# Turning the softmax sums of one row block, with two weight conversions placed later

## The chip, the cores and the metric

The kernel runs on one core of a Trainium2 chip. The core has five engines with a queue each: TensorE (PE in the rows; PEld is its loading of weights), VectorE (DVE), ScalarE (ACT), GpSimd (POOL) and SyncE (SP), which issues most of the DMAs. Each engine takes its instructions in the order in which they stand in its queue, and waits on semaphores for the others. The metric is the device time of one execution in microseconds; the median of three runs of the kernel before is 1201.55.

## What is computed

Capped attention, a gated MLP over its rows, and a mixture of experts with one expert a token. The part that matters here is the attention and the start of the MLP (all inputs are float32; `cap` is 30):

```python
scores = scale * np.matmul(q, k.transpose(0, 1, 3, 2))     # q, k, v: 4 x 12 x 448 x 64
scores = cap * np.tanh(scores / cap)
scores = scores - np.max(scores, axis=-1, keepdims=True)
attn = np.exp(scores)
attn = attn / (np.sum(attn, axis=-1, keepdims=True) + 1e-09)
x = np.matmul(attn, v)                                     # then 1792 rows of 12 * 64 = 768

rms = np.sqrt(np.mean(x * x, axis=-1, keepdims=True) + 1e-06)
xn = x / rms * rms_g
g = xn @ w_gate                                            # 768 x 1536
silu = g * (1.0 / (1.0 + np.exp(-g)))
x = (silu * (xn @ w_val)) @ w_out                          # 1536 x 768
```

After that come the routing of the 1792 rows to 8 experts with 224 places each, and two layers an expert; the change does not touch them.

## The kernel before

**Tiles and units.** The rows are worked in four blocks b of 448 (S), one for each element of the batch. The 12 heads of a block go in pairs: m counts 24 pairs, six a block, and a pair fills 128 partitions with two heads of 64. Scores are made transposed: 112 keys (T) on the partitions, 448 queries along the row, for both heads (a). A pair has four such key tiles; a unit u is two of them, m, i = divmod(u, 2). `scores(m, i)` makes the scores of a unit on PE into one of two PSUM tiles s_, and ACT makes tanh and exp of them into t_. `av(m, i)`, one unit later, multiplies v by t_ into a PSUM tile PS. All matmuls of the MLP split each float32 operand in a high and a low part (xh, xl; wh, wl) and sum three products (`mm3`).

**Sums of p.** The softmax needs 1 over the sum of t_ over all keys. For the first block of rows (m below 6) PE makes the sums by matmuls with ones beside those with v. From m = 6 on DVE adds the four tiles t_ into `ps` (L247, L250), and `fin(m)` sums its 112 partitions with two matmuls by ones, `ffb<-ps,ones`. These leave the sum of a head on all of its 64 partitions. DVE inverts the 128x448 tile (L270) and multiplies PS by it into oT (L274). The squares of oT, added up in ssq, give rms of a block.

**Weights.** The MLP's weights come as 64-bit floats in 18 pieces, 12 for gate and value columns and 6 for the output. They are made float32 by integer operations: a conversion (`convert`) handles half a piece: ACT makes u_ (L380), then DVE runs four operations (L381, L384 to L386). u_ has two buffers. `split_piece` then makes wh on ACT (L420) and wl on DVE (L422). `convert` runs ahead of need by `ahead`, at most three pieces (NR). A finished piece is also stored for the later blocks, which load it instead of converting it.

**Stages.** Stage 1 runs units 0 to 13, that is, block 0 and the start of block 1, with ten conversions in units 1 to 10; the order of PE's instructions is fixed there (`pinned`). Then `split_x(0)` makes xh and xl of block 0 and the body begins: `Driver.merge` mixes units of the next block with `gateval(0)`, which goes over 12 blocks of 128 gate and value columns (f), and with 16 conversions. A gate block takes two PSUM tiles, the gate's (j = 0) with six products by k, and then the value's (j = 1); DVE and ACT make silu of them. `rms` and `rms_rows` put 1/rms as RB behind the first products. Next come `second()`, the output projection of block 0 (`outproj`, whose results leave as xr) and the gates of block 1, and so on. In each, the order on an engine is set when the program is built: a scheduler with a timeline of its own puts what it takes to be ready first. PSUM for PS, gate tiles, sums and transposes is four tiles called ffb.

Of the kernel before, what the change touches and what calls it, by code (L numbers as in the profile page):

```python
# [10 lines left out]
F32 = mybir.dt.float32  # L11
F32R = mybir.dt.float32r
BF = mybir.dt.bfloat16
I32 = mybir.dt.int32
AF = mybir.ActivationFunctionType
# [4 lines left out]
B, H, S, D = 4, 12, 448, 64  # L20
# [3 lines left out]
T = 112  # L24
NQ = S // T
# [14 lines left out]
KD = DM // 128  # L40
KF = DF // 128
# [78 lines left out]
def program(tc, acap, general, qT, kT, v, wf64, g, wg2, w1, w2, out):  # L120

    nc = tc.nc
    drv = Driver()
    pe = Pe(tc)
    with ExitStack() as ctx:
# [6 lines left out]
        ident = const.tile([128, 128], F32, name="ident")  # L132
        make_identity(nc, ident)
        ones = const.tile([128, D], F32, name="ones")
# [32 lines left out]
        ff = ctx.enter_context(tc.tile_pool(name="ff", bufs=4, space=PSUM))  # L167
# [3 lines left out]
        wcv = actx.enter_context(tc.tile_pool(name="wcv", bufs=2))  # L171
        raw = actx.enter_context(tc.tile_pool(name="raw", bufs=3))
        pt = actx.enter_context(tc.tile_pool(name="pt", bufs=5))
        sm = actx.enter_context(tc.tile_pool(name="sm", bufs=2))
        ps_s = actx.enter_context(tc.tile_pool(name="ps_s", bufs=2, space=PSUM))

        RAW, MX, PT, PS, SU, OT, SQ = {}, {}, {}, {}, {}, {}, {}
# [50 lines left out]
        def halves(o_, w, x, first, last):  # L228

            for a in range(2):  # L230
                pe.matmul(o_[a * D:(a + 1) * D], w(a), x[:, a], start=first, stop=last, skip_group_check=True)

        def av(m, i):


            ts = [PT.pop((m, 2 * i + j)) for j in range(2)]
            if i == 0:
                PS[m] = ff.tile([128, S], F32, name="ffb")
                SU[m] = ff.tile([128, S], F32, name="ffb") if m < H // 2 else ts[0]
            for j, t_ in enumerate(ts):  # L240
                halves(PS[m], lambda a: RAW[m][2][:, a, 2 * i + j], t_, i + j == 0, i + j == 2)
            for j, t_ in enumerate(ts):
                if m < H // 2:
                    halves(SU[m], lambda a: ones[:T], t_, i + j == 0, i + j == 2)
                elif i + j == 1 and i == 0:
                    u_ = sm.tile([T, 2, S], F32, name="ps")
                    nc.vector.scalar_tensor_tensor(u_, SU[m], gcol[:T], t_, op0=OP.add, op1=OP.add)  # L247
                    SU[m] = u_
                elif i:
                    nc.vector.tensor_tensor(SU[m], SU[m], t_, op=OP.add)  # L250
            if i:
                RAW.pop(m)
                drv.later(1, lambda: fin(m))

        def square(b, o, x):
            if b:
                nc.scalar.activation(o, x, AF.Square)
            else:
                nc.gpsimd.tensor_tensor(o, x, x, op=OP.mult)

        def fin(m):
            b, c = divmod(m, H // 2)
            if c == 0:
                OT[b] = oTp.tile([128, KD, S], F32, name="oT")
            o_, u_ = PS.pop(m), SU.pop(m)
            rc = sm.tile([128, S], F32, name="rc")
            if b:
                p_ = ff.tile([128, S], F32, name="ffb")
                halves(p_, lambda a: ones[:T], u_, True, True)
                nc.vector.reciprocal(rc, p_)  # L270
            else:
                nc.vector.tensor_scalar(rc, u_, gsum, None, op0=OP.add)
                nc.vector.reciprocal(rc, rc)
            nc.vector.tensor_tensor(OT[b][:, c], o_, rc, op=OP.mult)  # L274
            x = OT[b][:, c]
            if c == 0:
                SQ[b] = ftmp.tile([128, S], F32, name="ssq", bufs=2)
                square(b, SQ[b], x)
            else:
                t_ = ftmp.tile([128, S], F32, name="sqt", tag="tmp", bufs=3)  # L280
                square(b, t_, x)
                nc.vector.tensor_tensor(SQ[b], SQ[b], t_, op=OP.add)

        def gate_constants():
# [10 lines left out]
        C_ATT = 24 * 2.24 * W_ATT  # L295

        def attention():
            load_pair(0, nc.sync)
            load_pair(1, nc.sync)
            load_half(NI - 1)  # L300
            gate_constants()
            for u in range(NH + 1):
                m, i = divmod(u, 2)
                if 0 < u < H - 1:
                    ahead(u - 1)
                if u in (H // 3, H // 2):
                    split_piece(u // 2 - 2)
                if m < NH // 2:
                    if i == 0 and general:
                        row_max(m)  # L310
                    if i == 0 and m + 2 < NH // 2:
                        load_pair(m + 2, nc.gpsimd)
                    scores(m, i)
                if u:
                    z, j = divmod(u - 1, 2)
                    av(z, j)
                yield 4.48
# [34 lines left out]
        HC = 6  # L352
# [15 lines left out]
        def convert(upto):  # L368

            while nh[1] <= min(upto, 2 * NP - 1):  # L370
                z, hf = divmod(nh[1], 2)
                load_half(nh[1])
                r_ = I64.pop(nh[1])
                if hf == 0:
                    WT[z] = wraw.tile([128, 12, 128], F32, name="r_", bufs=NR)
                u_ = wcv.tile([128, HC, 128], BF, name="u_", bufs=2)
                d_ = WT[z][:, hf * HC:(hf + 1) * HC]
                di = d_.bitcast(I32)
                hw, lw = r_[:, :, :, 1], r_[:, :, :, 0]
                tc.keep_in_program_order(nc.scalar.activation(u_, hw.bitcast(F32), AF.Abs))  # L380
                first = nc.vector.tensor_scalar(di, hw, 3, 0x3FFFFFF8, op0=OP.logical_shift_left,  # L381
                                                op1=OP.bitwise_and)
                tc.keep_in_program_order(first)
                nc.vector.scalar_tensor_tensor(di, hw, -0x40000000, di, op0=OP.bitwise_and, op1=OP.bitwise_or)  # L384
                nc.vector.scalar_tensor_tensor(di, lw, 29, di, op0=OP.logical_shift_right, op1=OP.bitwise_or)
                nc.vector.scalar_tensor_tensor(d_, u_, TINY, d_, op0=OP.is_ge, op1=OP.mult)  # L386
                load_half(nh[1] + NI)
                nh[1] += 1
                if hf:
                    nc.sync.dma_start(wf32[z], WT[z])  # L390
                    nxt[0] += 1
# [5 lines left out]
        def conversion(n):  # L397
            for _ in range(n):
                ahead(nh[1])
                yield 1  # L400
# [31 lines left out]
        def gateval(b):  # L432
            xh, xl = XN[b]
            for f in range(KF):
                z = GV0[b] + f
                split_piece(z + 1)
                wh, wl, r_ = WT.pop(z)
                order = [(j, k) for j in range(2) for k in range(KD)]
                if b == B - 2 and f == KF - 1:

                    order.sort(key=lambda jk: jk[1])
                ps = {}
                for i, (j, k) in enumerate(order):
                    if j not in ps:
                        ps[j] = ff.tile([128, S], F32, name="ffb")
                    mm3(ps[j], wh[:, 6 * j + k], wl[:, 6 * j + k], xh[k], xl[k], k, KD)
                    if f == 0 and i == 1 and b < B - 1:
                        rms(b)
                    if f == 0 and i == KD - 1:
                        rms_rows(b)  # L450
                    if i % 2:
                        yield 1.14
                    if (j, k) == (0, KD - 1):
                        o = ps[0]
                        th = ftmp.tile([128, S], F32, name="th", tag="tmp", bufs=3)
                        nc.vector.tensor_tensor(o, o, RB[b], op=OP.mult)
                        nc.scalar.activation(th, o, AF.Tanh, scale=0.5)
                        nc.vector.scalar_tensor_tensor(th, th, 1.0, o, op0=OP.add, op1=OP.mult)
                pool = tp if b < B - 1 else TP[0]
                th_ = pool.tile([128, S], F32R, name="tfh")  # L460
                tl_ = pool.tile([128, S], F32R, name="tfl")
                TF[b, f] = (th_, tl_)
                nc.vector.scalar_tensor_tensor(th, th, 0.5, ps[1], op0=OP.mult, op1=OP.mult)
                nc.scalar.activation(th_, th, AF.Copy)  # L464
                nc.gpsimd.tensor_tensor(tl_, th, th_.bitcast(F32), op=OP.subtract)  # L465
        C_GV = KF * 6 * 1.14
# [112 lines left out]
        att = attention()  # L579
# [1 line left out]
        drv.merge((islice(att, H + 2), 1))  # L581
        pe.pinned = False
        split_x(0)
        drv.merge((islice(att, H), C_ATT), (gateval(0), C_GV), (conversion(16), 16))
        split_x(1)
        drv.merge((islice(att, H), C_ATT), (second(), C_GV + C_OP), (conversion(20), 20))
        split_x(2)
# [391 lines left out]
```

## Time and profile before

| | |
|---|---|
| median of three runs (lowest to highest) | 1201.55 us (1195.22 to 1203.76) |
| profiled execution | 1201.41 us, span 1199.5 us |
| PE busy (matmuls) | 1126.7 us, 94% of the span |
| DVE busy | 770.9 us, 64% |
| ACT busy | 567.8 us, 47% |
| POOL busy | 207.4 us, 17% |
| mean granted clock of PE | 0.975 |

The shares are means over the whole span. The change touches the first 300 us, so the stages of that part are to be read by themselves: how many matmuls PE issues in a stretch, how long DVE is busy in it, and what ended PE's waits. Where a row counts several matmuls as one line, x4 means four passes through the array; a float32 matmul shows as two.

### The profile page before, as it was taken

What the parts mean: (1) busy time and instruction counts of PE and PEld (TensorE: products, weight loads), DVE (VectorE), ACT (ScalarE), POOL (GpSimd) and SP (SyncE); (2) the same over time, 40 slices, a digit from 0 to 9 for tenths busy, and PEclk for the clock granted to TensorE, in tenths of its full rate; (3) what the DMA queues carried; (4) which work ended last, traced back from release to release, by engine and by line L of the source; (5) the groups of instructions that cost most, each with busy time, mean ns of one, the idle gap of its engine ahead of it and who ended that gap; (6) DMA issues with size and microseconds to landing.
All of it is one profiled execution on the core that took longest, in us unless ns stands there. A gap on an engine that the chain in (4) does not pass through costs nothing. (4 is left out here: it accounts for less than half of the span.)

```text
span 1199.5 us, 14960 instructions
## 1 busy us (share of the span) xinstructions
PE 1126.7 (94%) x5830; PEld 867.8 (72%) x5830; DVE 770.9 (64%) x1118; ACT 567.8 (47%) x753; POOL 207.4 (17%) x188
## 2 busy tenths in 40 slices
PE   6988999989999999999899999999996999999995
PEld 2326666646677776577677899777775999999995
DVE  3996999998555665446575544255654666666661
ACT  5884667574344465543353333211002556666552
POOL 1222332210012221001112233311101101011000
PEclk8998999999999999999999999999998999999998
DMA  7661355547423333332232233410005666766640
GB/s 247 196 241 37 128 194 191 207 151 268 148 101 102 103 102 113 112 113 78 80 105 80 79 106 106 184 51 16 24 16 161 230 232 229 241 231 230 230 159 26
DMA packets 46113, 169.40 MB, mean 141 GB/s; under 512 B 5424, under 2 KB 16688, under 8 KB 46032
## 3 DMA queue, kind: packets, MB, share of 16 engines
q1 hardware_dynamic: 38896, 142.19, 35.2%
q0 software_dynamic: 7136, 26.16, 6.8%
q8 instruction: 48, 0.79, 0.3%
q14 instruction: 33, 0.27, 0.1%
HBM read 143.16 MB, written 25.17 MB: 140 GB/s over the span
## 5 line engine op out<-in xcount | busy, mean ns | idle before, releaser
L98 PE MATMUL ffb<-xh,wh 128*128 128x448 f32 x576 | 218.9, 380 | 7.0 <-DVE rc L270 4.5
L98 PE MATMUL ffb<-xl,wh 128*128 128x448 f32 x576 | 214.3, 372 | 0.0
L98 PE MATMUL ffb<-xh,wl 128*128 128x448 f32 x576 | 213.8, 371 | 0.0
L812 DVE TENSOR_TENSOR el<-mr,eh 128x1536 fp32r<-128x1536 f32 x64 | 112.5, 1758 | 72.8 <-ACT eh L811 72.8
L465 POOL TENSOR_TENSOR tfl<-th,tfh 128x448 fp32r<-128x448 f32 x48 | 103.6, 2158 | 293.3 <-ACT tfh L464 293.3
L98 PEld LDWEIGHTS ffb<-xh,wh 128*128 128x128 f32 x576 | 109.5, 190 | 43.3 <-issue 13.3
L98 PE MATMUL ffb<-tfh,wh 128*128 128x448 f32 x288 | 117.1, 406 | 4.7 <-ACT wh L420 3.2
L98 PE MATMUL ffb<-xg,eh 128*128 128x448 f32 x384 | 120.5, 375 | 0.0
L98 PEld LDWEIGHTS ffb<-xl,wh 128*128 128x128 f32 x576 | 109.6, 190 | 12.4 <-issue 2.8
L98 PEld LDWEIGHTS ffb<-xh,wl 128*128 128x128 f32 x576 | 109.4, 190 | 11.2 <-issue 0.7
L98 PE MATMUL ffb<-tfh,wl 128*128 128x448 f32 x288 | 108.7, 378 | 2.9 <-DVE wl L422 2.9
L811 ACT ACTIVATE eh<-mr 128x1536 fp32r<-128x1536 f32 x64 | 94.9, 1486 | 30.2 <-PE ffb L98 11.6
L98 PE MATMUL ffb<-tfl,wh 128*128 128x448 f32 x288 | 108.6, 377 | 0.0
L98 PE MATMUL ffb<-xg,el 128*128 128x224 f32 x384 | 91.9, 268 | 0.0
L98 PEld LDWEIGHTS ffb<-xg,el 128*128 128x128 f32 x384 | 73.7, 192 | 1.5
L98 PEld LDWEIGHTS ffb<-xg,eh 128*128 128x128 f32 x384 | 69.1, 190 | 3.8
L98 PEld LDWEIGHTS ffb<-tfh,wh 128*128 128x128 f32 x288 | 56.8, 197 | 19.8 <-issue 7.5
L98 PE MATMUL l<-el,hh 128*112 128x384 f32 x256 | 65.9, 338 | 0.0
L98 PE MATMUL l<-eh,hh 128*112 128x384 f32 x256 | 65.4, 342 | 0.0
L98 PE MATMUL l<-eh,hl 128*112 128x384 f32 x256 | 65.4, 336 | 0.0
L98 PEld LDWEIGHTS ffb<-tfh,wl 128*128 128x128 f32 x288 | 56.0, 195 | 9.7 <-DVE wl L422 3.4
L270 DVE RECIPROCAL rc<-ffb 128x448 f32<-128x448 f32 x18 | 53.1, 2953 | 13.1 <-PE ffb L98 13.1
(1164 smaller groups left out, 1957.7 us busy)
## 6 DMA issues: line engine op xcount, KB each, us to landing
mr<-w SPq DMA_DIRECT2D x64, 768.0 KB, 5.7
ih<-wf SPq DMA_DIRECT2D x36, 768.0 KB, 4.7
xrow<-xr SPq DMA_DIRECT2D x24, 224.0 KB, 2.5
gr<-wf SPq DMA_DIRECT2D x18, 256.0 KB, 2.9
wf<-r__191 SPq DMA_DIRECT2D x1, 768.0 KB, 5.6
wf<-r__264 SPq DMA_DIRECT2D x1, 768.0 KB, 7.6
wf<-r__341 SPq DMA_DIRECT2D x1, 768.0 KB, 3.2
wf<-r__418 SPq DMA_DIRECT2D x1, 768.0 KB, 3.3
```

Source lines behind the costliest of these rows:

```text
L98: return self.pin(self.tc.nc.tensor.matmul(*a, **k))
L270: nc.vector.reciprocal(rc, p_)
L465: nc.gpsimd.tensor_tensor(tl_, th, th_.bitcast(F32), op=OP.subtract)
L811: nc.scalar.activation(wh, r_, AF.Copy)
L812: sb = nc.vector.tensor_tensor(wl, r_, wh.bitcast(F32), op=OP.subtract)
```

## The change

Four things are changed in the first two stages.

1. For pairs 6 to 11 (`turned`, the second block of rows) the sums are taken with the tiles' columns turned onto partitions: `invert` runs eight matmuls that have 112 columns of ps as weights and one column of ones as data, into eight spare columns of the PSUM tile PS (which is now 512 wide). DVE inverts the 112x8 result, ACT spreads each number over 64 elements (`rw`, 112x512), and two steps later `fin` turns the four 112x128 parts back by PE transposes; ACT copies them to rc. The multiplication by rc stays. All other pairs of later blocks keep the old way.
2. The conversions in stage 1 end after unit 8 instead of 10, the merge of the body asks for 20 instead of 16, and u_ has three buffers.
3. The first gate block of block 0 goes by k with both tiles side by side, so that each xh, xl serves gate and value at once; rms and rms_rows stand accordingly later.
4. The square of pair 5 moves from GpSimd to ACT.

```diff
+        def turned(m):
+            return H // 2 <= m < H
+
+        def turned_sums(m, t_):
+            for i in range(NQ):
+                for a in range(2):
+                    z = S + 2 * i + a
+                    pe.matmul(PS[m][:T, z:z + 1], t_[:, a, i * T:(i + 1) * T], ones[:T, :1], start=False, stop=True,
+                              skip_group_check=True)
...
             if i == 0:
-                PS[m] = ff.tile([128, S], F32, name="ffb")
+                PS[m] = ff.tile([128, 512], F32, name="ffb")
...
-                drv.later(1, lambda: fin(m))
+                drv.later(1, partial(invert if turned(m) else fin, m))
...
-            if b:
+            if m >= H // 2 - 1:
                 nc.scalar.activation(o, x, AF.Square)
...
+        def invert(m):
+            turned_sums(m, SU[m])
+            ri = sm.tile([T, NQ, 2], F32, name="ri")
+            nc.vector.reciprocal(ri.rearrange("p i a -> p (i a)"), PS[m][:T, S:S + 2 * NQ])
+            SU[m] = sm.tile([T, NQ, 2 * D], F32, name="rw", bufs=1)
+            nc.scalar.activation(SU[m].rearrange("p i (a d) -> p i a d", a=2),
+                                 ri[:, :, :, None].to_broadcast([T, NQ, 2, D]), AF.Copy)
+            drv.later(2, partial(fin, m))
...
+                p_ = ff.tile([128, S], F32, name="ffb")
+                if turned(m):
+                    for i in range(NQ):
+                        pe.transpose(p_[:, i * T:(i + 1) * T], u_[:, i], ident[:T, :T])
+                    nc.scalar.activation(rc, p_, AF.Copy)
+                else:
+                    halves(p_, lambda a: ones[:T], u_, True, True)
+                    nc.vector.reciprocal(rc, p_)
...
-                if 0 < u < H - 1:
+                if 0 < u < H - 3:
                     ahead(u - 1)
...
-                u_ = wcv.tile([128, HC, 128], BF, name="u_", bufs=2)
+                u_ = wcv.tile([128, HC, 128], BF, name="u_", bufs=3)
...
-                if b == B - 2 and f == KF - 1:
+                late = b == 0 and f == 0
+                if late or (b == B - 2 and f == KF - 1):
                     order.sort(key=lambda jk: jk[1])
...
-                    if f == 0 and i == 1 and b < B - 1:
+                    if f == 0 and i == (2 * KD - 3 if late else 1) and b < B - 1:
                         rms(b)
-                    if f == 0 and i == KD - 1:
+                    if f == 0 and i == (2 * KD - 2 if late else KD - 1):
                         rms_rows(b)
...
-        drv.merge((islice(att, H), C_ATT), (gateval(0), C_GV), (conversion(16), 16))
+        drv.merge((islice(att, H), C_ATT), (gateval(0), C_GV), (conversion(20), 20))
```

The scheduler moves instructions with this. On PE at the seam of stage 1 and the body, behind the last scores of unit 13 (in these rows xh_638, xl_639 are the parts for k = 0 before, xh_620, xl_621 in the change; the numbers only tell tiles apart), before:

```order
L98 MATMUL ffb<-t__598,v__460 64x448 x2
L98 MATMUL ffb<-t__599,v__460 64x448 x2
L98 MATMUL s__668<-q__531,k__532 112x448 x2
L98 MATMUL ffb<-t__625,v__460 64x448 x2
L98 MATMUL s__669<-q__531,k__532 112x448 x2
L98 MATMUL ffb<-t__626,v__460 64x448 x2
L98 MATMUL ffb<-ps,ones 64x448 x2
L98 MATMUL ffb<-xh_638,wh 128x448
L98 MATMUL ffb<-xl_639,wh 128x448
```

and now:

```order
L98 MATMUL ffb<-t__580,v__460 64x448 x2
L98 MATMUL ffb<-xh_620,wh 128x448
L98 MATMUL ffb<-xl_621,wh 128x448
L98 MATMUL ffb<-xh_620,wl 128x448
L98 MATMUL ffb<-xh_624,wh 128x448
L98 MATMUL ffb<-xl_625,wh 128x448
L98 MATMUL ffb<-xh_624,wl 128x448
L98 MATMUL ffb<-t__581,v__460 64x448 x2
L98 MATMUL ffb<-xh_628,wh 128x448
L98 MATMUL ffb<-xl_629,wh 128x448
```

Before, all gate products stand behind the sums of pair 6 (`ffb<-ps,ones`). Now twelve stand ahead of the scores of unit 14, the first eight of them in these rows, and five more follow before pair 6's sums.

Further on in the same stretch PE now has the way back of pair 6 (rw) and the rows of rms behind the last products of the first gate block, with scores of units 15 to 17 among them, and the second gate block's first product behind:

```order
L98 MATMUL ffb<-xh_640,wl 128x448
L98 MATMUL s__781<-q__513,k__514 112x448 x2
L98 MATMUL s__782<-q__513,k__514 112x448
L101 MATMUL ffb<-ident,rw 128x112 x4
L98 MATMUL s__782<-q__513,k__514 112x448
L98 MATMUL s__875<-q__568,k__569 112x448 x2
L98 MATMUL ffb<-ones,ssq 112x1 x4
L98 MATMUL s__876<-q__568,k__569 112x448 x2
L98 MATMUL s__985<-q__568,k__569 112x448 x2
L101 MATMUL ffb<-ident,RR 128x112 x4
L98 MATMUL ffb<-xh_620,wh 128x448
```

Before, only the scores s of unit 15 stood in this stretch; those of s__875, s__876 and s__985 came behind gate products of the next block.

On DVE at the start of the output projection, ahead of the first xr. Before (r__1609 is the 13th piece of the weights, r__1705 the 14th):

```order
L381 TENSOR_SCALAR r__1705<-ih 128x768
L250 TENSOR_TENSOR ps<-ps,t__1937 112x896
L384 SCALAR_TENSOR_TENSOR r__1705<-ih,r__1705 128x768
L250 TENSOR_TENSOR ps<-ps,t__1938 112x896
L422 TENSOR_TENSOR wl<-r__1609,wh 128x1536
L381 TENSOR_SCALAR r__1705<-ih 128x768
L385 SCALAR_TENSOR_TENSOR r__1705<-ih,r__1705 128x768
L506 TENSOR_TENSOR xr<-ffb,RR 112x512
```

and now (r__1795 is the 14th piece, r__1925 the 15th, r__2043 the 16th):

```order
L450 TENSOR_TENSOR wl<-r__1795,wh 128x1536
L409 TENSOR_SCALAR r__2043<-ih 128x768
L414 SCALAR_TENSOR_TENSOR r__1925<-u__1926,r__1925 128x768
L409 TENSOR_SCALAR r__1925<-ih 128x768
L412 SCALAR_TENSOR_TENSOR r__2043<-ih,r__2043 128x768
L263 TENSOR_TENSOR ps<-ps,t__2021 112x896
L535 TENSOR_TENSOR xr<-ffb,RR 112x512
```

Before, the 13th piece was split and the 14th in the making when the first xr came; now the 14th is split, and the 15th and 16th are in the making. Behind about 340 us the order of the engines is as before, but for one pair that changes places on DVE.

## Rows read from the trace of the kernel before

**Rows 1.** Stretches: us; busy us (instructions) PE, PEld, DVE, ACT, POOL; PEclk, DMA, GB/s.
```profile
54.84:85.50 30.66, 25.48 (x120) 8.12 (x120) 30.10 (x32) 24.95 (x26) 5.08 (x8) 1.00 0.71 248
85.50:110.20 24.70, 21.47 (x95) 12.78 (x94) 18.42 (x21) 13.49 (x17) 7.43 (x9) 0.86 0.27 91
...
97.50:110.20 12.70, 12.70 (x59) 10.42 (x58) 7.35 (x9) 5.33 (x8) 2.18 (x3) 0.81 0.18 54
110.20:245.00 134.80, 131.56 (x601) 88.26 (x601) 128.82 (x141) 87.05 (x102) 39.91 (x26) 0.99 0.48 166
245.00:340.00 95.00, 86.22 (x391) 56.60 (x388) 73.81 (x83) 47.05 (x53) 7.35 (x11) 0.96 0.56 186
345.00:445.00 100.00, 100.00 (x479) 76.20 (x478) 59.30 (x61) 48.55 (x58) 26.77 (x20) 1.00 0.31 105
```

**Rows 2.** Waits, 7 to 97 us, ACT: who waited for whom, us, times, longest.
```profile
ACT u__522 L380 <- DVE r__418 L386: 1.7, 1, 1.7
...
ACT u__419 L380 <- DVE r__341 L386: 1.5, 1, 1.5
```

**Rows 3.** Timeline (start, us, instruction, [idle <-releaser]): first scores of units 8, 12, 13.
```profile
54.84 1.01 PE L98 MATMUL s__464<-q__308,k__309 64*112 64x448 f32 x4 [0.17 <-ACT t__433 L219]
...
80.65 1.01 PE L98 MATMUL s__592<-q__458,k__459 64*112 64x448 f32 x4
...
85.50 1.01 PE L98 MATMUL s__619<-q__458,k__459 64*112 64x448 f32 x4
```

**Rows 4.** Timeline: a conversion on DVE to the next one's start, then the seam.
```profile
75.64 0.55 DVE L381 TENSOR_SCALAR r__491<-ih 128x768 int32<-128x768 int32 x1
76.22 0.96 DVE L384 SCALAR_TENSOR_TENSOR r__491<-ih,r__491 128x768 int32<-128x768 int32 x1
...
79.16 0.55 DVE L381 TENSOR_SCALAR r__491<-ih 128x768 int32<-128x768 int32 x1
...
95.83 1.76 PE L98 MATMUL ffb<-ps,ones 112*64 112x448 f32 x4 [3.23 <-DVE ps L250]
...
96.97 0.62 DVE L282 TENSOR_TENSOR ssq<-ssq,sqt 128x448 f32<-128x448 f32 x1 [0.82 <-POOL sqt L259]
97.51 0.68 DVE L348 SCALAR_TENSOR_TENSOR xl<-oT,gt,xh 128x448 fp32r<-128x448 f32 x1
```

**Rows 5.** Timeline: the first product of the second gate block.
```profile
110.19 0.36 PE L98 MATMUL ffb<-xh,wh 128*128 128x448 f32 x1
```

**Rows 6.** DVE's reciprocals: groups of 97.5 to 244.5 us, and a timeline row.
```profile
L270 DVE RECIPROCAL rc<-ffb 128x448 f32<-128x448 f32 x6 | 17.7, 2950 | 0.6 <-PE ffb L98 0.6
...
4.49 0.15 DVE L139 RECIPROCAL qs<-acap 128x1 f32<-128x1 f32 x1
```

**Rows 7.** Timeline of PE: the matmuls of rms and the transposes of its rows.
```profile
329.91 0.85 PE L98 MATMUL ffb<-ones,ssq 128*112 128x1 f32 x8
330.62 0.45 PE L98 MATMUL ffb<-xh,wh 128*128 128x448 f32 x1
...
337.83 0.57 PE L101 MATMUL ffb<-ident,RR 112*128 112x112 f32 x4
```

**Rows 8.** ACT's copies: a timeline row, and a group of 97.5 to 244.5 us.
```profile
108.30 0.53 ACT L336 ACTIVATE RB<-ffb 128x448 f32<-128x448 f32 x1
...
L257 ACT ACTIVATE sqt<-oT 128x448 f32<-128x448 f32 x5 | 2.9, 571 | 7.9 <-DVE oT L274 7.9
```

**Rows 9.** Waits, 245 to 340 us, PE: us, times, longest.
```profile
PE ffb L98 <- ACT wh L420: 3.2, 2, 1.6
PE ffb L98 <- DVE wl L422: 2.9, 1, 2.9
PE ffb L98 <- DVE th L458: 1.5, 1, 1.5
```

More of the change, by code (lines that the diff above doesn't have):

```diff
@@ L237, in av @@
             if i == 0:
-                PS[m] = ff.tile([128, S], F32, name="ffb")
+                PS[m] = ff.tile([128, 512], F32, name="ffb")
                 SU[m] = ff.tile([128, S], F32, name="ffb") if m < H // 2 else ts[0]
             for j, t_ in enumerate(ts):
-                halves(PS[m], lambda a: RAW[m][2][:, a, 2 * i + j], t_, i + j == 0, i + j == 2)
+                halves(PS[m][:, :S], lambda a: RAW[m][2][:, a, 2 * i + j], t_, i + j == 0, i + j == 2)
             for j, t_ in enumerate(ts):
@@ L252, in av, with square @@
                 RAW.pop(m)
-                drv.later(1, lambda: fin(m))
-        def square(b, o, x):
-            if b:
+                drv.later(1, partial(invert if turned(m) else fin, m))
+        def square(m, o, x):
+            if m >= H // 2 - 1:
                 nc.scalar.activation(o, x, AF.Square)
@@ L264, in fin @@
                 OT[b] = oTp.tile([128, KD, S], F32, name="oT")
-            o_, u_ = PS.pop(m), SU.pop(m)
+            o_, u_ = PS.pop(m)[:, :S], SU.pop(m)
             rc = sm.tile([128, S], F32, name="rc")
[L267 to L271, printed above, removed]
+            if b == 0:
                 nc.vector.tensor_scalar(rc, u_, gsum, None, op0=OP.add)
                 nc.vector.reciprocal(rc, rc)
+            else:
[4 more added lines that the diff above has]
+                    nc.scalar.activation(rc, p_, AF.Copy)
+                else:
+                    halves(p_, lambda a: ones[:T], u_, True, True)
+                    nc.vector.reciprocal(rc, p_)
             nc.vector.tensor_tensor(OT[b][:, c], o_, rc, op=OP.mult)
@@ L277, in fin @@
                 SQ[b] = ftmp.tile([128, S], F32, name="ssq", bufs=2)
-                square(b, SQ[b], x)
+                square(m, SQ[b], x)
             else:
                 t_ = ftmp.tile([128, S], F32, name="sqt", tag="tmp", bufs=3)
-                square(b, t_, x)
+                square(m, t_, x)
                 nc.vector.tensor_tensor(SQ[b], SQ[b], t_, op=OP.add)
```

## The prediction

> **What bounds the kernel now.** I read the time by stages first, then what ended the waits in each, then single rows.
>
> The profiled execution took 1201.41 us, of which the span is 1199.5; the median of the three runs is 1201.55, so the sum below can be set against either. TensorE (PE) is busy for 94% of the span, but the table by stages shows where it is not well fed [rows 1]. From 345 to 445 us, where VectorE (DVE) has work for only 59 us, PE issues 479 matmuls in 100.0 us, 0.209 us each; I use this as the price of one in this mix. At that price the 601 matmuls of 110.2 to 245 us need 125.6 us and take 134.8 (9.2 lost), and the 391 of 245 to 340 us need 81.7 and take 95.0 (13.3 lost). In those two stretches DVE is busy 128.8 and 73.8 us, and late in the first stage, from 54.84 to 85.5 us, 30.1 of 30.7. So up to about 300 us DVE works nearly without a break, and PE waits for what it makes late. From 340 us on the order of the engines is the same in both kernels but for one swap on DVE, so what is won by then stays won.
>
> How DVE's lateness reaches PE in the first stage: ACT, about to make u_ for a conversion, stood waiting for a u_ buffer, which is freed by the last DVE operation of the conversion two before. There are four such waits of 1.5 to 1.7 us [rows 2]. Behind it in ACT's queue stand the tanh and exp of the scores, and PE has only two score buffers. Units of attention follow each other at 4.85 us where nothing waits (80.65 to 85.50), but the four from 54.84 to 80.65 took 25.8 us instead of 19.4 [rows 3]. At the seam between the stages PE then waits 3.23 us for p's sums, with the first gate products queued behind, and the last xl is made only at 97.51 [rows 4]. PE's granted clock is 0.81 in the mean there, so at its lower level (1.2 GHz) for part of the time [rows 1].
>
> **The change, part by part.**
>
> *Two conversions later, three u_ buffers, products by k.* A conversion costs DVE 3.5 us (75.64 to 79.16) [rows 4] and ACT 0.9. Two of them leave the first stage: 7.0 us of DVE. DVE's work there is unbroken, so the last xl is ready near 97.5 - 7.0 = 90.5 us. With three buffers and no conversion behind the eighth, ACT has none of the four waits, and unit 13's scores start near 54.84 + 5 x 4.85 = 79.1 instead of 85.50. From there to the first product of the second block of gate columns, 110.19 [rows 5], PE takes 24.7 us for 95 matmuls [rows 1], which at 0.209 are 19.9. In the order of the change the stretch also holds 12 matmuls of scores that came later (2.5 us), and the first turned pair (+1.0, below): 23.4 us. Gate products stand where the 3.23 us wait was. What is new is that PE needs ACT's copy of the turned sums, its copy back and RB, one behind the other; I allow 3 us for these. The stretch ends at 79.1 + 23.4 + 3 = 105.5: 4.7 us sooner and 2.5 us of scores further on, 7.2 in all. If the clock falls as it does before (0.81 over 12.7 us costs 2.4), it is 4.8. I take 6; the bounds are 4.8 and, without the 3 us, 10. The conversions land where DVE has room, busy 7.35 of 12.7 us from 97.5 to 110.2 [rows 1]; without that room they would cost DVE 7 us in the stage behind. SyncE's queue carries the same loads two conversions later, with nobody new waiting for them. One square goes from GpSimd, where it held DVE's ssq up by 0.82 us [rows 4], to ACT for 0.57 us [rows 8].
>
> *Six pairs turned.* DVE loses six reciprocals of 2.95 us [rows 6] and gains six of 112x8. The small one has no row; it lies between 0.15 us (a reciprocal of one column [rows 6]) and 2.95, and with eight columns against 448 I take 0.2. That is 16.5 us of DVE, 13.8 of them behind 110 us. PE loses two matmuls with ones, four passes or 0.84 us, and gains eight one-column matmuls and four transposes. The nearest row is rms: four one-column matmuls, 8 passes, 0.71 us to the next matmul [rows 7]. So 16 passes take 1.42. Four transposes show 0.57 with their tail [rows 7]; I take 0.45. Net +1.0 us a pair, 6 in all. ACT gains two copies, near 0.53 and 0.65 us (0.57 for 448 elements, scaled to 512) [rows 8], 1.2 us a pair; it is busy 87 of 134.8 us [rows 1], which hides them unless PE waits for one.
>
> The price of the one-column passes is where the gain turns. The Trainium skill (TensorE: Matmul & The Clock Gate, section Back-to-back issue gap) gives matmuls of 1 to 64 columns a floor of about 25 ns; by that the 16 passes would cost 0.4 us, a pair nothing net, and the result would be near 1184. The trace shows 0.71/8 = 89 ns a pass, and I go by the row.
>
> *The body, 110 to 245 us.* DVE needs 128.8 - 13.8 and some 2 us of the moved conversions for which the room does not suffice: 117 us. PE needs 125.6 + 5 x 1.0 = 130.6. So PE becomes the bound, and the most to be had is 134.8 - 130.6 = 4.2 us. Not all of PE's waits will go: weights, p's sums and PSUM tiles still come in turn. I take half, 2 us. If nothing of the 9.2 is won back, the stage is 5 us longer.
>
> *The output projection, 245 to 340 us.* PE waits for wh, wl and th, 7.6 us in four waits [rows 9], and the mean clock of 0.96 [rows 1] costs up to 3.8. Both come from DVE being late with conversions. In the changed order DVE has converted one piece more before the first xr and begun the next two, and it arrives with some 10 us less behind it. I take 3.5 us; the bounds are 0 (the wait moves to the next late piece) and 9.
>
> **Sum.** 6 + 2 + 3.5 = 11.5 us; 1201.4 - 11.5 = 1189.9, say 1190.
>
> **Rivals.**
>
> *PE is full.* For: in the body PE reads as busy 131.6 of 134.8 us [rows 1]. Taken at its word there are 3.2 us to win and 5.0 to add; with all its present waits the body is 5 us longer. Against: 479 matmuls in 100 us read as full too, at a higher rate. Then 6 - 5 + 1 are won: 1199.5. The Trainium skill (Trainium Kernel Development and Optimization, section Performance Expectations) calls matmul busy time a bad metric, because matmuls are pipelined. By that, the trace agrees: 601 in 134.8 and 479 in 100.0 us both read as nearly full.
>
> *All of it.* The seam gives 9, the body 4.2, the projection 8: 1180. For: 22.5 us are lost in the two stretches, and one-column passes below 89 ns would help. Against: PE, in order, has waits that are not DVE's.
>
> *The way back is too long (slower).* PE meets the transposes in order, with gate products queued behind, before ACT has written the turned sums: DVE's small reciprocal may stand behind a wl, ACT's copy behind tanh, exp or wh, six times over. At a wait like that of the seam, 3.23 us [rows 4], this costs 19 us, and 2.4 each for the clock behind it, 14 more: 1190 + 33 = 1223. The gain is gone from 11.5/6 = 1.9 us a pair, without the clock. Against: the order sets scores or gate products between the sums and the way back.
>
> *Nothing moves.* The waits of the first stage pass to DVE's next late result; 2 of the 6 stay and the rest cancels: about 1200.
>
> **Chances.** The forecast, 1184 to 1196: 0.50. PE full: 0.18. All of it: 0.17. Nothing moves: 0.07. Slower: 0.08. Less than 1% (1189.5 to 1213.6) can hardly be told from no change here. Half of the forecast's own range lies below 1189.5, so faster is 0.25 + 0.17 = 0.42; slower by over 1% is 0.06, and within 1% 0.52. The range leaves out the slower case and the lower part of "all of it": 1181 to 1201.
>
> **What would show it.** Units 9 to 13 at 4.85 us and no wait for u_ in the first stage; the second gate block's first product near 105.5 us; eight one-column matmuls at 1.4 us, and transposes of rw with no wait ahead of them; body and projection shorter by 2 and 3.5 us; a constant shift from 340 us on. It would be wrong if PE waited ahead of most of those transposes, if the one-column matmuls were well off 1.4 us, or if DVE still had no break before 300 us.

## The result, and the profile after

The changed kernel takes 1184.13 us (median of four runs, 1181.26 to 1189.33) beside 1200.63 for the kernel before on the same chip: a ratio of 0.9866, interval 0.9839 to 0.9894, so 12.7 to 19.3 us less. On a second occasion it was 0.9890 (0.9861 to 0.9919). The profiled execution, 1189.33 us, is the slowest of the four, 12.0 us of span below before's.

The page's head, and the table by stages in the columns of [rows 1], cut at the same places of the program (unit 8, unit 13, first product of the second gate block, first product of the output projection, then a stretch in which both kernels run the same order):

```profile
PE 1130.0 (95%) x5926; PEld 876.9 (74%) x5926; DVE 754.1 (64%) x1118; ACT 572.6 (48%) x766; POOL 206.8 (17%) x187
```
```profile
53.49:78.46 24.97, 24.66 (x123) 8.29 (x121) 24.55 (x25) 21.93 (x23) 5.18 (x8) 1.00 0.73 247
78.46:108.23 29.77, 24.26 (x123) 13.91 (x121) 25.31 (x31) 19.66 (x23) 9.67 (x8) 0.94 0.32 98
108.23:243.61 135.38, 134.88 (x675) 96.38 (x673) 122.10 (x152) 91.64 (x115) 36.67 (x27) 0.99 0.58 195
243.61:332.00 88.39, 88.39 (x409) 59.70 (x410) 67.42 (x73) 45.94 (x52) 7.02 (x11) 1.00 0.50 164
332.00:432.00 100.00, 100.00 (x478) 76.23 (x477) 58.96 (x61) 48.82 (x57) 26.59 (x20) 1.00 0.32 106
```

DVE has breaks now (122.1 of 135.4 us in the body, where [rows 1] had 128.8 of 134.8), and PE has none: in the projection it is busy for the whole stretch at full clock. Behind it nothing moved, 478 matmuls in 100 us as before. From 110 to 340 us a single wait of PE is left, in the columns of [rows 9]:

```profile
PE ffb L98 <- DVE th L487: 0.5, 1, 0.5
```

The seam, to be laid beside [rows 3], [rows 4] and [rows 5]. The first scores of units 8, 12 and 13; the first gate product; the sums of pair 6 (x16), rw, and the rows of rms (RR):

```profile
53.49 1.01 PE L98 MATMUL s__464<-q__308,k__309 64*112 64x448 f32 x4
...
73.61 1.01 PE L98 MATMUL s__574<-q__458,k__459 64*112 64x448 f32 x4
...
78.46 1.01 PE L98 MATMUL s__601<-q__458,k__459 64*112 64x448 f32 x4
...
81.05 0.47 PE L98 MATMUL ffb<-xh,wh 128*128 128x448 f32 x1
...
89.82 1.64 PE L98 MATMUL ffb<-ones,ps 112*112 112x1 f32 x16
...
97.08 0.60 PE L101 MATMUL ffb<-ident,rw 112*128 112x112 f32 x4
...
101.02 1.01 PE L98 MATMUL s__985<-q__568,k__569 64*112 64x448 f32 x4
107.54 1.01 PE L101 MATMUL ffb<-ident,RR 112*128 112x112 f32 x4 [5.51 <-POOL RR L356]
108.23 0.72 PE L98 MATMUL ffb<-xh,wh 128*128 128x448 f32 x1
```

Units 8 to 13 follow each other at 4.99 us, the gate products fill the place of the old wait, and no transpose of rw has a wait ahead of it. But PE now stands still for 5.51 us at another place. What it waited for is GpSimd's power for 1/rms; beside it, DVE at the same time:

```profile
102.19 5.30 POOL L356 TENSOR_TENSOR RR<-RR,mhalf 112x4 f32<-112x4 f32 x1 [2.19 <-DVE RR L355]
```
```profile
101.95 0.16 DVE L355 TENSOR_SCALAR RR<-ffb 112x4 f32<-112x4 f32 x1
102.02 0.95 DVE L413 SCALAR_TENSOR_TENSOR r__806<-ih,r__806 128x768 int32<-128x768 int32 x1
102.89 0.95 DVE L412 SCALAR_TENSOR_TENSOR r__688<-ih,r__688 128x768 int32<-128x768 int32 x1
103.75 1.09 DVE L263 TENSOR_TENSOR ps<-ps,t__788 112x896 f32<-112x896 f32 x1
104.76 0.95 DVE L413 SCALAR_TENSOR_TENSOR r__688<-ih,r__688 128x768 int32<-128x768 int32 x1
105.62 0.95 DVE L414 SCALAR_TENSOR_TENSOR r__806<-u__807,r__806 128x768 f32<-128x768 bf16 x1
```

The same power took 1.04 us in the kernel before, at 103.16, when DVE had nothing but one multiplication. Here DVE runs two conversions in turn, the second of the two that were moved (r__688) and the first of the next piece (r__806), which stood at 117.78 us before; the power ends 0.92 us after the last row shown.

A turned pair in the body: the sums until the next matmul 1.60 us, the transposes until the next 0.48; ri, rw and rc on DVE and ACT:

```profile
147.06 1.73 PE L98 MATMUL ffb<-ones,ps 112*112 112x1 f32 x16
148.66 0.45 PE L98 MATMUL ffb<-xh,wh 128*128 128x448 f32 x1
...
155.45 0.60 PE L101 MATMUL ffb<-ident,rw 112*128 112x112 f32 x4
155.93 0.47 PE L98 MATMUL ffb<-xh,wh 128*128 128x448 f32 x1
```
```profile
151.17 0.20 DVE L278 RECIPROCAL ri<-ffb 112x8 f32<-112x8 f32 x1
```
```profile
151.40 0.63 ACT L280 ACTIVATE rw<-ri 112x512 f32<-112x512 f32 x1 [4.18 <-DVE ri L278]
...
159.55 0.53 ACT L298 ACTIVATE rc<-ffb 128x448 f32<-128x448 f32 x1
```

### The profile page after: what moved, and what is told of

The parts are those of the page before. It is cut to its first block, busy times and chain, and to the rows that moved or that the text cites. A ratio compares the mean times of both kernels' runs of the same rounds, so it can differ in the third digit from the quotient of the medians.

```text
span 1187.5 us, 15155 instructions
## 1 busy us (share of the span) xinstructions
PE 1130.0 (95%) x5926; PEld 876.9 (74%) x5926; DVE 754.1 (64%) x1118; ACT 572.6 (48%) x766; POOL 206.8 (17%) x187
## 4 chain that ended last, share of the span: by engine, by line
PE 74%; issue 10%; DVE 10%; DMA 2%; ACT 1%; POOL 1%; SPq 0%; POOLq 0%; DVEq 0%; ACTq 0%
PE ffb L98 58%; PE l L98 7%; PE ffb L101 3%; PE pb L98 2%; DMA ih<-wf 1%; DVE wl L450 1%; POOL out L932 1%; DVE rc L292 1%; DVE xr L535 0%; DMA mr<-w 0%; POOL RR L356 0%; DVE ps L263 0%; DMA xr<-xrow,idx 0%; DVE xl L376 0%; DVE kc L720 0%
## 5 line engine op out<-in xcount | busy, mean ns | idle before, releaser
L494 POOL TENSOR_TENSOR tfl<-th,tfh 128x448 fp32r<-128x448 f32 x48 | 99.7, 2076 | 304.1 <-ACT tfh L493 304.1
L492 DVE SCALAR_TENSOR_TENSOR th<-th,ffb 128x448 f32<-128x448 f32 x48 | 29.7, 618 | 47.5 <-PE ffb L98 47.0
```

## The experiments

All ratios are to the kernel before on the same chip, with 95% intervals. The three points are starts in each kernel's profiled execution: the second gate block's first product, the output projection's first product, and the first scores of unit 34, behind which the order is shared. From there to the end of the span the fourteen executions take 826.3 to 831.2 us, and 830.4 and 829.1 in the two of the change, so a difference of a few us is read at unit 34 and not from the span.

| kernel | ratio | gate block 2 | projection | unit 34 |
|---|---|---|---|---|
| before | 1 | 110.19 | 250.16 | 370.39 |
| the change | 0.9866 (0.9839 to 0.9894) | 108.23 | 243.61 | 357.06 |
| the change again | 0.9890 (0.9861 to 0.9919) | 105.98 | 242.35 | 355.81 |
| rms earlier | 0.9865 (0.9836 to 0.9893) | 101.55 | 237.32 | 350.78 |
| no side-by-side block | 0.9865 (0.9842 to 0.9888) | 102.69 | 237.83 | 351.29 |
| no turned pair | 0.9872 (0.9843 to 0.9901) | 101.87 | 237.55 | 353.98 |
| conversions back | 0.9887 (0.9861 to 0.9913) | 109.01 | 244.44 | 358.09 |
| turned sums alone | 0.9923 (0.9906 to 0.9940) | 107.19 | 243.71 | 358.37 |
| third u_ buffer alone | 0.9971 (0.9956 to 0.9986) | 108.39 | 247.11 | 367.51 |
| DVE's reciprocals back | 0.9958 (0.9942 to 0.9975) | 107.58 | 253.62 | 365.35 |
| sums twice | 1.0036 (1.0022 to 1.0050) | 109.46 | 260.48 | 373.82 |
| sums twice, apart | 0.9949 (0.9932 to 0.9966) | 106.76 | 251.55 | 363.65 |
| pair 6 alone | 0.9934 (0.9913 to 0.9955) | 102.78 | 240.26 | 358.07 |
| pairs 6, 10, 11 | 0.9882 (0.9859 to 0.9905) | 100.66 | 237.46 | 353.43 |

**The change again.** No edit.

> The changed kernel once more, nothing edited. Its first profiled execution took 1189.3 us, 5 us more than its median of 1184.1, and shows GpSimd's power of RR in 5.30 us at 102.19 (the same operation took 1.04 us in the kernel before), with PE waiting 5.51 us behind it. Theory A: the order of instructions decides it. From 102.02 to 106.57 DVE runs operations with two SBUF inputs one behind the other, and GpSimd stands still until the first break; the power takes 5.0 to 5.6 us again. Theory B: a stray of that one execution; the power takes about 1.0 us, PE's wait there is about 1.2, and the second gate block starts near 104. Median 1182 to 1186 by both.

```profile
102.69 2.55 POOL L356 TENSOR_TENSOR RR<-RR,mhalf 112x4 f32<-112x4 f32 x1 [2.18 <-DVE RR L355]
```

PE waited 2.76 us. Neither number: not 5.3 and not 1.0. The order of instructions is the same and DVE as busy, so the order alone does not fix the length: here the power ends beside DVE's third instruction, not behind its fifth. The wait is real both times, but its size varies by some 3 us from one execution to the next.

**rms earlier.**

```diff
-                    if f == 0 and i == (2 * KD - 3 if late else 1) and b < B - 1:
+                    if f == 0 and i == (1 if late else 1) and b < B - 1:
```

> rms of block 0 is placed behind the first products of the first gate block instead of behind its ninth step; nothing else is edited. Its matmuls with ones then follow pair 6's turned sums at about 91 us, and GpSimd's power runs 6 us sooner. Theory A (DVE's two-input operations hold GpSimd up): the power may still be long, until DVE's break near 96.5, but the transposes of RR no longer wait; the wait of 5.5 us goes but for about 1 us behind ACT's copy of rw, and the time falls by 4 to 5, to about 1180. Theory B (a stray): the power is not what the median pays for; the time falls by 1 us or less, 1183 to 1184. Theory C: what PE wins there it loses to DVE's next late piece of weights: the second gate block starts 4 us sooner, and the time is the same within 2 us.

```profile
93.64 1.28 POOL L356 TENSOR_TENSOR RR<-RR,mhalf 112x4 f32<-112x4 f32 x1 [3.07 <-DVE RR L355]
```
```profile
100.08 0.60 PE L101 MATMUL ffb<-ident,RR 112*128 112x112 f32 x4
```

The wait is gone, and so is the lower clock that followed it in the change (0.50 from 107.54 to 111.36). Unit 34 starts 5.0 and 6.3 us before that of the change's two profiles, and the median is 3.5 us below the change measured with it (1184.97 to 1188.48). The intervals of the two overlap, so the trace shows the gain and the times only agree with it. A is right on the wait, but not on the power, which is short here, nor on 1180. C falls: the gain is carried to unit 34.

**No turned pair.**

```diff
-            return H // 2 <= m < H
+            return False
```

> The changed kernel with the sums of pairs 6 to 11 made the old way (two matmuls with ones, 2.95 us of DVE a pair); the conversions stay two later, u_ has three buffers, the first gate products stay side by side. By the prediction DVE has 16.5 us more to do before 245 us and, with two conversions more behind 97 us, sets the time again, while PE has 6 us less: the body and the output projection fall back by what they won beyond the seam, 1184 + 10 = 1194 (1190 to 1198). If the turned sums cost PE more than they save (rival: PE is full), it is faster than the change: 1178 to 1182. If the turned sums carry the whole gain, it is 1200 or more, slower than the kernel before, since DVE has 7 us of conversions more in the body.

The prediction's answer, 1190 to 1198, fails: 1185.47, level with the change. PE's waits from 85 to 345 us, then body and projection:

```profile
PE ffb L98 <- ACT wh L448: 4.7, 1, 4.7
PE ffb L98 <- DVE ps L263: 2.6, 1, 2.6
PE ffb L98 <- DVE th L487: 1.8, 2, 1.0
```
```profile
101.87:237.55 135.68, 132.63 (x616) 87.38 (x614) 135.58 (x155) 94.02 (x114) 38.41 (x31) 1.00 0.56 188
237.55:327.00 89.45, 83.51 (x391) 57.75 (x392) 70.23 (x77) 43.04 (x49) 6.16 (x9) 0.98 0.56 186
```

DVE works for 135.58 of the body's 135.68 us and PE hardly waits for it there: DVE just keeps up. In the projection it does not: PE waits 4.7 us for wh at 252.68, and from the projection's first product to unit 34 it takes 116.4 us, where the change takes 113.45. That the two are level all the same has a cause outside the sums: GpSimd's power takes 1.04 us here, at 99.86, so the change's wait for it is missing too, and the second gate block starts 4.1 and 6.4 us sooner than in the change's two profiles. The fairer partner is the kernel with rms earlier, which has no such wait either. The first scores of unit 34, there and here:

```profile
350.78 0.92 PE L98 MATMUL s__2848<-q__2396,k__2397 64*112 64x448 f32 x4
```
```profile
353.98 0.92 PE L98 MATMUL s__2764<-q__2312,k__2313 64*112 64x448 f32 x4
```

By the traces the six turned pairs are worth 3.2 us beside the other parts. The times, 1184.97 and 1185.47, don't resolve it.

**Conversions back.**

```diff
-                if 0 < u < H - 3:
+                if 0 < u < H - 1:
...
-        drv.merge((islice(att, H), C_ATT), (gateval(0), C_GV), (conversion(20), 20))
+        drv.merge((islice(att, H), C_ATT), (gateval(0), C_GV), (conversion(16), 16))
```

> The changed kernel with the conversions where they were (ten in the first stage, sixteen asked for in the body); three buffers for u_, turned sums and side-by-side products stay. By the prediction (DVE's unbroken work in the first stage sets the seam) units 9 to 13 follow each other at more than 5.5 us again in the mean, the first gate product comes 5 to 7 us later than in the change, and the time rises by 4 to 6 us: 1188 to 1190. If the buffers alone took the waits away (ACT's waits for u_), the units stay near 4.9 us and the time rises by 2 us or less. If the two conversions only change places with other work of DVE, it is 1184 as well.

The time is 1187.52, and its interval covers both of the change's ratios: the forecast of 4 to 6 us more is not met. The first scores of units 8 and 12, the first gate product, and ACT's wait:

```profile
54.24 1.01 PE L98 MATMUL s__464<-q__308,k__309 64*112 64x448 f32 x4
...
80.29 1.01 PE L98 MATMUL s__592<-q__458,k__459 64*112 64x448 f32 x4
...
87.73 0.47 PE L98 MATMUL ffb<-xh,wh 128*128 128x448 f32 x1
```
```profile
69.19 0.91 ACT L408 ACTIVATE u__522<-ih 128x768 bf16<-128x768 f32 x1 [2.63 <-DMA ih<-wf]
```

Units 8 to 12 take 26.05 us again with three buffers, and the first gate product comes 6.7 us later than in the change. The waits for a u_ buffer are gone, but ACT waits for the next load ih instead, and SyncE can issue that load only when DVE has left an ih buffer (it waits for DVE's work on r__418 twice, 8.7 us in all). So DVE still sets the stage, as the prediction had it, by another way. That the 26.05 us are nearly those of before is partly chance: 0.63 is the mean clock from 71.05 to 80.29 here, and the kernel before with a third buffer alone, which has the same conversions, takes 24.13. Yet unit 34 loses only 1.0 to 2.3 us: GpSimd's power takes 1.04 us here, at 107.24, since the conversions no longer run beside it. What the move won in the first stage it mostly lost again at the power.

**The third u_ buffer alone**, on the kernel before.

```diff
-                u_ = wcv.tile([128, HC, 128], BF, name="u_", bufs=2)
+                u_ = wcv.tile([128, HC, 128], BF, name="u_", bufs=3)
```

> The kernel before with three buffers for u_ and nothing else; instructions change places only from the body on. Theory U (in the body DVE and ACT stop one another at u_, and the third buffer lets DVE run without a break): DVE's busy share of the body rises from 0.96 to 0.99 or more, body and output projection are 5 to 8 us shorter together, 1193 to 1196. Theory S (the prediction: DVE has too much to do, and only less work for it helps): DVE's work is the same and the time as well, 1199 to 1203. The first stage is the same by both within 1 us, since DVE is busy there 30.1 of 30.7 us.

Between the two: 3.5 us by the ratio (1.7 to 5.3), and DVE's share of the body stays at 0.957 (132.72 of 138.72 us; before, 134.00 of 139.97). U is too large, S too small, and the projection wins nothing (120.4 us to unit 34, as before). That the first stage would stay the same within 1 us is missed as well: units 8 to 12 take 24.13 us, 1.7 less than before, and the second gate block starts 1.8 us sooner.

**The turned sums alone**, on the kernel before (parts 2 to 4 of the change left out).

> The kernel before with the turned sums of pairs 6 to 11 and nothing else: conversions, two buffers for u_, the order of the first gate block and the square stay as before. By the prediction's sum body and projection win 2 + 3.5 us (DVE has 16.5 us less to do), less 1 us for the first pair: 1195 to 1197. If a turned pair only passes the time from DVE to PE (theory P, after the run without turned sums came out level with the change): 1199 to 1203. If the way back stalls PE (slower): 1206 or more, with waits ahead of the transposes of rw.

1189.99, a ratio that means 9.2 us less (7.2 to 11.3): more than the prediction's own 5.5, and far from level. Its body and projection, in the columns of [rows 1]:

```profile
107.19:243.71 136.52, 133.15 (x677) 95.22 (x675) 127.21 (x153) 93.97 (x116) 35.37 (x27) 1.00 0.56 183
243.71:333.00 89.29, 88.66 (x407) 61.21 (x408) 67.86 (x74) 45.78 (x52) 6.58 (x10) 0.98 0.52 169
```

So the turned sums are worth 9 us on the kernel before, and by the trace 3 beside the other parts. The parts don't add: the turned sums alone bring 9.2 us, the change without them some 15, and the whole change 13 to 16. That they are two cures for one complaint, DVE's lateness, fits this; it isn't shown by itself.

**No side-by-side block.**

```diff
-                late = b == 0 and f == 0
+                late = False
```

> The changed kernel with the first gate block made as before, the gate tile's six products first and the value tile's behind; all else as in the change. The prediction gave this part no price of its own: it fills the wait for p's sums. If it does, PE meets the later xl sooner and waits for them: the xl of k = 5 is made at 89 us and PE would want it near 86, so the second gate block starts 2 to 4 us later per unit of work done and the time is 1188 to 1191. If rms standing earlier (GpSimd's power no longer waited for) outweighs that: 1182 to 1186, as with rms placed earlier.

1182.47, the low answer. With the gate tile first, rms stands earlier and the power is over long before its rows are wanted (1.28 us at 93.67). PE does not wait for the later xl. Beside the kernel with rms earlier (the same ratio; unit 34 at 351.29 and 350.78) the order by k brings half a us at most. In the change it costs 4.5 to 5.8 us up to unit 34, since it carries rms to a later place; the times don't resolve that either.

**Sums twice.** `turned_sums(m, SU[m], 8)` behind the first, `z = S + off + 2 * i + a`.

> The changed kernel with the eight one-column matmuls of each of the six turned pairs made a second time, into eight further spare columns that nobody reads: 48 matmuls more on PE, no work more on any other engine. By the prediction (PE is the bound of the body and a pair's passes cost 1.42 us) all of it shows: 6 x 1.4 to 1.5 = 8.5 to 9 us, 1193 to 1197 beside a change of 1185 to 1188. If PE still has slack in the body, as where it waits for DVE, it shows less than 4 us. If one-column matmuls cost 25 ns a pass behind one another, 2.4 us.

All three numbers are too small: 18 to 20 us beside the change. A doubled run in the body, then the clock in the stretch behind it (the column behind POOL's):

```profile
150.69 3.77 PE L98 MATMUL ffb<-ones,ps 112*112 112x1 f32 x32
154.32 0.72 PE L98 MATMUL ffb<-xh,wh 128*128 128x448 f32 x1
154.84 0.57 PE L98 MATMUL ffb<-xl,wh 128*128 128x448 f32 x1
```
```profile
150.69:154.32 3.63, 3.63 (x34) 3.63 (x33) 3.63 (x5) 0.13 (x1) 3.42 (x1) 0.87 0.01 2
154.32:158.20 3.88, 3.88 (x12) 3.45 (x12) 3.88 (x5) 0.63 (x1) 3.78 (x2) 0.50 0.59 171
```

The passes cost about what the single ones did, 3.1 to 3.6 us a doubled run, and behind this one TensorE runs at its lower level (1.2 GHz): 12 matmuls in 3.88 us.

**Sums twice, apart.** The second eight matmuls a step later:

```diff
+            drv.later(1, partial(turned_sums, m, su, 8))
             drv.later(2, partial(fin, m))
```

> As the run with the turned sums made twice, but the second eight matmuls of a pair stand a step later, ahead of the transposes of rw, with other work of PE between: two runs of 1.5 us in place of one of 3.0. The same 48 matmuls are added. Doubled behind one another they cost the body 15.1 us, 3.0 a pair, and in three of the five places the granted clock behind the run of 3.1 to 3.6 us was at its lower level for 3 to 6 us. Theory K (the passes cost 1.5 us a pair, the rest is the clock that falls behind a long run of one-column matmuls): here the clock stays, and the time rises by 6 x 1.5 = 9 us beside the change, to 1194 to 1198. Theory R (a pair's sums simply cost 3 us more when doubled): 1202 to 1206 again.

1194.62, theory K: 7 to 10 us beside the change's two ratios, for 9 of passes. Two stretches of lower clock remain in it (96 to 111 and 128 to 135 us), so K is right on the size but not clean: both times the clock fell behind a pair's second run of 16 passes (96.18 and 126.87 us).

**DVE's reciprocals back.**

```diff
                     nc.scalar.activation(rc, p_, AF.Copy)
+                    rd = sm.tile([128, S], F32, name="rc")
+                    nc.vector.reciprocal(rd, rc)
```

> The changed kernel with DVE's old work put back on top: behind ACT's copy of a turned pair, DVE inverts a 128x448 tile (2.95 us) that nobody reads, ahead of the multiplication into oT. DVE has 6 x 2.95 = 17.7 us more, PE and ACT the same as in the change. By the prediction (DVE's lateness sets the time) body and projection fall back by what DVE's relief gave: 2 + 3.5 to 7 us, 1191 to 1196. If PE alone bounds the changed body (DVE has work for 122 of its 135 us), the reciprocals lie in DVE's breaks, and the time rises by 3 us or less: 1185 to 1190.

```profile
PE ffb L101 <- POOL RR L358: 4.7, 1, 4.7
PE s__2027 L98 <- ACT t__1899 L219: 2.4, 1, 2.4
PE s__2028 L98 <- ACT t__1900 L219: 2.2, 1, 2.2
PE ffb L101 <- ACT rw L280: 1.4, 1, 1.4
```
```profile
107.58:253.62 146.04, 140.05 (x682) 98.32 (x680) 138.23 (x161) 94.61 (x119) 34.35 (x27) 0.97 0.54 182
```

1194.50, by the prediction: the ratio is 0.007 to 0.009 above the change's, 8 to 11 us. PE has the same passes and the body is 10 us longer than the change's 135.38 and 136.37; from the projection's first product on nothing is lost. The wait for RR lies ahead of the body, the other three at its end, at 247.58, 251.85 and 231.22, and the clock is 0.97 in the mean. The relief of DVE is what pays for the turned sums; that PE alone is the bound is refuted. One thing the run does not part: each reciprocal also stands between a pair's rc and its oT, so it delays that chain besides filling DVE's time.

**Pair 6 alone; pairs 6, 10 and 11**, both with rms earlier.

```diff
-            return H // 2 <= m < H
+            return m == 6
```

> The changed kernel with only pair 6 turned, and rms of block 0 behind the first products as in the run with rms earlier. Pair 6 fills the seam; the five others, which cost PE some 1.2 us each, go back to DVE. If PE alone bounds the body: 5 x 1.2 = 6 us less than with rms earlier, 1178 to 1180. If DVE, with 13.8 us more, makes PE wait as without any turned pair (4.7 us for wh at the start of the output projection, some 3 in the body): nothing won, 1184 to 1187.

> As the one before with pairs 6, 10 and 11 turned: pair 6 for the seam, 10 and 11 to have DVE 5.5 us ahead where it was late for the output projection. Three pairs at 1.2 us less for PE than in the run with rms earlier. If the wait of 4.7 us at the projection goes: 3.6 us less than there, 1180 to 1182. If PE waits elsewhere for DVE instead: 1184 to 1186.

1191.18 and 1184.78. Fewer turned pairs don't win. With pair 6 alone PE waits nine times from 200 us on, 8.6 us in all, and its mean clock in the projection is 0.96:

```profile
240.26:330.00 89.74, 85.29 (x388) 58.30 (x387) 69.41 (x74) 42.59 (x48) 8.74 (x10) 0.96 0.55 187
```

The edit differs from the kernel with rms earlier by pairs 7 to 11 alone, and those two intervals do not meet (0.9913 to 0.9955, 0.9836 to 0.9893): turning the five is worth 6 to 8 us here, 7.3 at unit 34. The kernel with no turned pair gives 3.2 for all six. Why pair 6 alone is 5.7 us slower than that kernel, whose DVE has more to do, I can't say: the scheduler sets another order in seam and body, and no run holds that order fixed. Of all these kernels none is measurably faster than the change.

## Why the prediction was right, and where it was not

**Time.** 1190.0 was forecast, from a sum of 11.5 us against one execution; the profiles show 12.0 and 14.6 (13.3 and 14.6 at unit 34), and the medians 16.5 and 13.4 us. The range held 1184.13. "Within 1%" was given more weight than "faster by over 1%"; the interval of the first measurement lies just beyond 1%, that of the second reaches back to 0.8%. The undersized term is the projection.

**Seam, forecast 6.** The second gate block came at 108.23 and 105.98, which with the 2.5 us of scores moved ahead of it is 4.5 and 6.7. Right inside it: unit 13 at 78.46 (79.1 forecast), the last xl at about 89.6 (90.5), no wait for a u_ buffer. The failed step is "PE needs ACT's copy of the turned sums, its copy back and RB, one behind the other; I allow 3 us for these". The copies cost PE nothing. The wait lay on GpSimd's power in the making of RB, 5.51 and 2.76 us, and it was made by a step that I had booked as free: "the conversions land where DVE has room". I asked what they cost DVE there, not whom they hold up. That the seam came out near 6 is therefore partly luck: the 3 us were set aside for copies that cost nothing, and went to a wait that was not foreseen.

**Body, forecast 2.** From 139.97 to 135.38 and 136.37 us; less the scores that now stand ahead of it, 2.1 and 1.1. PE did become the bound: no wait of it is left in the body. A pair's sums took 1.5 to 1.6 (1.42 forecast), the transposes 0.4 to 0.5 (0.45), the two matmuls they replace 0.9 (0.84): net 1.0 to 1.2 against 1.0. ri was 0.20, rw 0.63, rc 0.53, all as taken.

**Projection, forecast 3.5, bounds 0 to 9.** From its first product to unit 34, 120.23 became 113.45: 6.8 us, in both profiles. Mechanism right, size too small: 3.5 is under a third of the 11.4 us that the prediction lists there in waits (7.6) and clock (3.8), and it gives no reason for that share. Of the waits of [rows 9] 0.5 us is left, for th, and the clock is 1.00. Two of them had a stretch of lower clock behind them (0.88 in the mean from 261 to 275 us, 0.86 from 303 to 315), so a wait that goes brings its clock back too. The stage won 6.8 and not 11 in part because 12 matmuls more stand between the two points; the rest is open.

**What the prediction did not see** is that the parts replace each other. It credited the turned sums with 13.8 us of DVE's relief on top of everything else. Alone they bring 9 us; taken out of the change they are worth 3 by the trace (6 to 8 for five pairs, by the kernel with pair 6 alone), because with the other parts DVE works for 135.58 of the body's 135.68 us and just keeps up, while PE saves six pairs.

**Rivals.** "PE is full" was half right: PE is fed without a break, and each pass more shows (sums twice, apart). But each reciprocal given back shows as well, so the body stands where both engines are at their limit. "All of it" gave 1180 and is what the kernels with no wait at the seam come near to, 1182.5 and 1185. "The way back is too long" did not happen: no wait ahead of rw in the change. Nor did "nothing moves": the gain of the first stage reaches unit 34.

**Open.** How much the later conversions bring by themselves (no run has them alone), what the turned sums are worth in place, between 3 and 8 us, and why pair 6 alone is slower than none.

## What to carry to other kernels

Two parts that relieve the same engine are not to be added: price each with the other in place, and check whether the relieved engine is still late. Before a run without a part is called level, look at each stage: two differences can cancel, as the turned sums and the wait for GpSimd did here. When work is moved to where an engine "has room", look at what else runs then, above all a GpSimd operation that another engine waits for. And count a wait together with the clock behind it.

## What the hardware showed that I had not expected

GpSimd's power of 112x4 elements took 1.04 us beside an idle DVE, and 2.55 and 5.30 where DVE ran the steps of two conversions in turn, starting 0.86 to 1.01 us apart with no break; in three of the experiments it was 1.69 (twice) and 4.39 beside such a row of steps. Beside the steps of one conversion, each waiting for the one before (starts at 94.05 and 95.05, 0.96 us each, in the kernel with rms earlier), it took 1.28. The Trainium skill (SBUF — State Buffer, section Who interferes with whom) says that a DVE instruction with two SBUF inputs contends with a GpSimd instruction that reads SBUF, and that the ports they share are an exclusive lock. The traces agree in part: the power is long just where DVE runs such instructions without a break, and over several of them, five in one execution and three in the next at the same order. But in four of these five cases it ended 0.98 to 1.00 us after DVE had started an addition to ps, which has two SBUF inputs as well, so as the profile dates it the power ran beside that one (in the change again, 104.26 to 105.34, with the power's end at 105.24). What lets it in, no run shows.

A run of one-column matmuls reads as busy PE, yet behind four of the five unbroken doubled runs the granted clock was at its lower level for a time, 0.50 from 154.32 to 158.20, with no wait ahead of it. Behind the single runs of 1.6 us in the change's body it stayed at 1.00, but in the kernel with the sums apart it fell twice behind such a run. Doubling 8 us of such work in the body cost 14.7 to 15.6.
